# A token router's counting rounds on full 128 by 128 arrays, in a fused attention and mixture-of-experts kernel

## The chip, the cores and the metric

The kernel runs on one core of a Trainium2 chip, as one program. The metric is the device time in microseconds (us) of one launch. Times inside the program are read from one profiled execution, taken by the hardware profiler; "span" is the time from its first to its last instruction. Engines are named as in the profile: PE (matrix multiplies), PEld (the loading of the stationary operand, which overlaps PE), DVE (vector engine), ACT (scalar engine), POOL (GpSimd), SP (the queue that issues most transfers).

## What is computed

Attention through 32 memory slots per head gives 4608 tokens of 512 features. A router then hands every token to one of eight experts with room for 576 tokens each, each expert is a two-layer network, and a dense two-layer network follows.

```python
def _moe_ref(x, w_gate, w1, w2):
    N, D = x.shape
    E = w_gate.shape[1]                 # 8
    cap = N // E                        # 576
    logits = x @ w_gate
    order = np.argsort(-logits.flatten())
    assigned, counts = -np.ones(N, np.int64), np.zeros(E, np.int64)
    for idx in order:                   # best logit first
        tok, e = idx // E, idx % E
        if assigned[tok] >= 0 or counts[e] >= cap:
            continue
        assigned[tok] = e
        counts[e] += 1
    ...
    for e in range(E):
        mask = assigned == e
        out[mask] = np.maximum(x[mask] @ w1[e], 0.0) @ w2[e]
    return out

def _moe2_ref(x, w_in, w_out):
    h = x @ w_in
    return (h * np.clip(h + 3.0, 0.0, 6.0) / 6.0) @ w_out
```

## The kernel before

**Stages.** The first 180 us or so are attention. What follows is recorded by a planner: `mm` (L617, L618) emits one matmul of the expert or dense layers and moves a model clock `CK.now` on by the cost that `fp16` gives; after each matmul, `run` lets background tasks (Python generators) emit their instructions once the model clock has reached the time that each has yielded. So every engine executes in order a stream that the planner wrote, and the costs in the code (`CK.now += 0.3`, `HOP`, `LATE`) set where a task's instructions stand in it. L567 is the helper through which the tasks' DVE, ACT and POOL instructions go, L618 that of the matmuls.

**The main stream on PE.** For each pair P of experts come `l1`, `l2` of expert 2P, `l1`, `l2` of expert 2P+1 (192 matmuls each of 288 columns, written to the tiles `p` from `xt` or `h`), and then `l34`, the dense network on these 1152 tokens. `l34` takes 48 steps; a step is twelve matmuls of 384 columns (`p<-yt,wi`) and nine of 512 columns (`acc<-wo,h`). The dense weights are turned from fp32 bit patterns into scaled pairs of fp16 by the task `dense_piece` (32 pieces, four DVE instructions on the tile `cva` for each) in the first pair's time.

**The router.** `routes` runs `route(k)` for k = 0 to 7, one after the other; `R_OK` lets k = 1 start at the beginning of the experts, 2 and 3 in `l34` of the first pair, 4 and 5 in that of the second, 6 and 7 in that of the third. A route finds the expert that fills up at the highest threshold and the tokens that it takes. Routes 0 to 6 do so in eight rounds (`NST`): in a round, DVE compares the best logit `V` of each token (128 partitions by 36 token tiles) with 15 thresholds `TH` (the tile `C`), PE counts for each threshold and expert how many tokens pass (`C` against the one-hot choice `Bo`), DVE asks which counts reach 576 (`FL`), PE sums those flags and copies the sum to all partitions (`p2`), and DVE makes the next 15 thresholds from it. Route 0 has rounds of 36 small matmuls (L785). From route 1 on a round has three groups on PE:

- L795: nine matmuls, each with four token tiles, 60 columns of `C` as the stationary operand and 32 columns of `Bo` moving; the 15 by 8 blocks on the diagonal of the 60 by 32 result hold the counts of four tile groups;
- L804: four matmuls that add these blocks, with slices `idh` of an identity (60 partitions by 15), after DVE has copied the result out of the accumulator as `CS` (L800);
- L813: one matmul of 15 partitions, ones against `FL`.

After the rounds the route counts once more (L855), which gives the expert's number and lets `weights` fetch its weights (`w_issue`, on the POOL queue); it then ranks its tokens (L882, L883) and makes their index list (six groups L952). `gathers` fetches the tokens' rows by this list (`xg`) and transposes them on PE (`xp`, L623) to the tiles `xt` that `l1` reads; it does so for expert k once `l1` of expert k-1 is emitted. For k of two and more, `LATE` (1.6) adds slack to the planned times: half of it before each L795 group.

## Time and profile before

| | us |
|---|---|
| median of 3 runs | 1510.31 (1505.42, 1511.45, 1510.31) |
| the profiled execution itself | 1503.65 |
| its span, first to last instruction | 1501.6 |
| PE busy in the span | 1397.4 (93%) |
| DVE busy | 835.3 (56%) |
| ACT busy | 732.6 (49%) |
| POOL busy | 487.8 (32%) |

The profiled execution took 2.05 us more than its span, and lies 6.7 us (0.4%) under the median of the three runs. PE is the engine with the largest share, but shares are averages over stages: before 180 us (attention) and from there to about 437 us PE has gaps, after that nearly none. A row of the timeline gives start, duration, engine, line, what is written from what, and in square brackets how long the engine had been idle and for whom it waited. The duration of a merged row of matmuls runs to the end of the last one, which overlaps the next row's start; what a group takes from the stream is therefore read from starts.

### The profile page before, as it was taken

The page shows a single profiled execution, that of the slowest core. Times are in us where ns is not written, and L with a number is a line of the kernel's source. Part 1 is how long each engine was busy: PE and PEld are TensorE (multiplying, and loading weights), DVE is VectorE, ACT ScalarE, POOL GpSimd, SP SyncE. Part 2 cuts the span into 40 slices and gives each one's busy share as a digit, 9 for nine tenths or more (in the row PEclk, how much of TensorE's full clock was granted, in tenths as well). Part 3 has the DMA queues.
Part 4 walks back from the last instruction along what each step waited for, and adds up shares of the span by engine and source line. Part 5 has one row for each costly group of instructions (what it writes and reads, how often), then busy time and mean ns, then how long its engine had stood idle before and what let it go on. Part 6 is the DMA issues. An engine that isn't in the chain of part 4 may idle for free.

```text
span 1501.6 us, 26275 instructions
## 1 busy us (share of the span) xinstructions
PE 1397.4 (93%) x10506; PEld 931.4 (62%) x10506; DVE 835.3 (56%) x1985; ACT 732.6 (49%) x1419; POOL 487.8 (32%) x555
## 2 busy tenths in 40 slices
PE   4778886898889999999999999999999999999997
PEld 3667764777444555997555558875555588755553
DVE  4788967889995775553146755522459335221111
ACT  3667655577763563452335634523346445233332
POOL 3565305134553443301233532102325421023232
PEclk9989996999999999999999999999999999999999
DMA  9866587355310221200001311100013211000000
GB/s 299 293 231 201 158 273 248 118 185 167 114 43 22 82 84 57 86 28 2 1 22 57 109 57 51 64 1 1 22 57 110 71 39 62 1 0 22 1 21 21
DMA packets 65913, 130.67 MB, mean 87 GB/s; under 512 B 5248, under 2 KB 35968, under 8 KB 65792
## 3 DMA queue, kind: packets, MB, share of 16 engines
q1 hardware_dynamic: 49808, 74.48, 15.0%
q0 software_dynamic: 15168, 52.96, 10.9%
q8 instruction: 82, 1.34, 0.4%
q10 hardware_dynamic: 816, 1.57, 0.3%
q14 instruction: 39, 0.32, 0.1%
HBM read 110.12 MB, written 18.87 MB: 86 GB/s over the span
## 4 chain that ended last, share of the span: by engine, by line
PE 67%; DVE 14%; ACT 5%; issue 5%; DMA 4%; POOL 2%; SPq 0%; ACTq 0%; POOLq 0%; DVEq 0%
PE p L618 39%; PE acc L618 21%; DVE cva L567 4%; DMA xg<-xd,ix 2%; PE xa L420 1%; DMA ph<-in_phi_dram 1%; PE kvp L191 1%; DMA wst<-in_moe_w_dram,ei 1%; DVE w L567 1%; ACT h L567 1%; PE rtp L795 1%; DVE pm L138 1%; PE xp L623 1%; DVE h L567 1%; POOL h L567 1%
## 5 line engine op out<-in xcount | busy, mean ns | idle before, releaser
L618 PE MATMUL acc<-wo,h 128*128 128x512 f16 x1728 | 418.1, 379 | 5.2 <-ACT h L567 4.3
L618 PE MATMUL p<-yt,wi 128*128 128x384 f16 x2304 | 417.6, 327 | 0.0
L567 POOL TENSOR_TENSOR h<-h,h 128x384 f16<-128x384 f32 x192 | 187.3, 976 | 634.5 <-ACT h L567 492.6
L618 PEld LDWEIGHTS <-w 128*128 128x128 f16 x3072 | 339.1, 121 | 49.1 <-issue 4.4
L618 PEld LDWEIGHTS <-wi 128*128 128x128 f16 x2304 | 219.2, 98 | 156.0 <-issue 1.2
L567 ACT ACTIVATE h<-p,half_c,inv 128x384 f32<-128x384 f32 (+1 forms) x256 | 143.9, 587 | 278.5 <-PE p L618 271.2
L618 PEld LDWEIGHTS <-h 128*128 128x128 f16 x1728 | 163.5, 98 | 174.1 <-ACT h L567 6.0
L567 DVE SCALAR_TENSOR_TENSOR h<-h,p 128x384 f32<-128x384 f32 x192 | 105.9, 551 | 290.0 <-ACT h L567 282.7
L618 PE MATMUL p<-xt,w 128*128 128x288 f16 x1536 | 198.8, 289 | 3.7 <-DVE h L567 3.5
L618 PE MATMUL p<-h,w 128*128 128x288 f16 x1536 | 196.3, 287 | 4.3 <-DVE w L567 3.7
L567 ACT ACTIVATE h<-h 128x384 f16<-128x384 f32 x192 | 100.1, 521 | 135.7 <-DVE h L567 131.9
L567 DVE SCALAR_TENSOR_TENSOR h<-p,h 128x288 f16<-128x288 f32 x128 | 57.4, 455 | 73.6 <-ACT h L567 73.5
L567 DVE SCALAR_TENSOR_TENSOR w<-wst,s,w 128x512 f16<-128x512 f32 x124 | 96.1, 806 | 2.2 <-ACT w L567 2.2
L567 POOL DMA_INDIRECT wst<-in_moe_w_dram,ei x64 | 68.7, 1073 | 87.0 <-DVE scn L567 33.5
L567 ACT ACTIVATE h<-p 128x288 f16<-128x288 f32 x128 | 51.7, 410 | 90.8 <-PE p L618 90.8
L567 ACT ACTIVATE w<-wst,s 128x512 f16<-128x512 f32 x124 | 82.5, 712 | 7.1 <-DVE s L567 6.2
L567 DVE SCALAR_TENSOR_TENSOR cva<-dst,cva 128x512 int32<-128x512 int32 (+1 forms) x96 | 82.7, 881 | 0.5 <-ACT dst L567 0.3
L567 DVE TENSOR_REDUCE ym<-y 128x1 f32<-128x288 f32 x64 | 28.8, 450 | 91.5 <-ACT y L567 91.3
L567 ACT ACTIVATE wscr<-wst 128x1024 bf16<-128x1024 f32 x64 | 67.3, 1052 | 13.3 <-DMA wst<-in_moe_w_dram,ei 12.6
L567 ACT ACTIVATE y<-p 128x288 f32<-128x288 f32 x64 | 26.1, 407 | 96.6 <-PE p L618 95.1
L567 POOL DMA_INDIRECT xg<-xd,ix x35 | 37.2, 1064 | 75.9 <-PE xp L623 49.7
L191 PE MATMUL kvp<-kvt,A 128*64 128x128 f32 x576 | 46.0, 315 | 7.3 <-ACT A L170 3.3
(313 smaller groups left out, 1558.4 us busy)
## 6 DMA issues: line engine op xcount, KB each, us to landing
dst<-in_moe_w_out_dram SPq DMA_DIRECT2D x26, 512.0 KB, 4.3
qt<-in_q_dram SPq DMA_DIRECT2D x8, 1024.0 KB, 11.5
dq<-in_moe_w_in_dram SPq DMA_DIRECT2D x16, 512.0 KB, 5.7
xd<-xs SPq DMA_DIRECT2D x32, 256.0 KB, 5.5
kvt<-in_k_dram SPq DMA_DIRECT2D x7, 1152.0 KB, 9.1
kvt<-in_v_dram SPq DMA_DIRECT2D x7, 1152.0 KB, 11.8
dst<-in_moe_w_in_dram SPq DMA_DIRECT2D x15, 512.0 KB, 4.0
ph<-in_phi_dram SPq DMA_DIRECT2D x8, 576.0 KB, 9.8
```

The source lines that it names most:

```text
L138: nc.vector.tensor_reduce(pm, PH[b].rearrange("p h (r m) -> p h m r", m=M), axis=AX.X, op=OP.max)
L191: nc.tensor.matmul(p[i * 64:(i + 1) * 64, g, 0:128], A[:, hp, r, :], KV[b][:, :, hp, r * 64:(r + 1) * 64], start=(r == 0), stop=(r == R - 1))
L420: nc.tensor.matmul(p[r, g], AT[u][:, half, g, r], VB[b][:, g], start=True, stop=True)
L567: r = f(*a, **kw)
L618: nc.tensor.matmul(o, l, r, start=start, stop=stop)
L623: nc.tensor.transpose(o, i, idn)
L795: nc.tensor.matmul(p[:60, :32], C[:, 4 * t:4 * t + 4].rearrange("p t n -> p (t n)"), Bo[:, 4 * t:4 * t + 4].rearrange("p t e -> p (t e)"), ...
```

## The change

Counting groups from route 1 on are made eight token tiles wide, with sixteen columns of `C` for each tile in place of fifteen; `C` and `Bo` are padded with zeros to 40 tiles, allocated once and cleared once on POOL. Five matmuls with a stationary operand of 128 by 128 and 64 moving columns take the place of nine. DVE no longer copies the result: it multiplies it by a mask `MK` that keeps the diagonal blocks (`CM`) and adds the eight blocks of a row (`CR`). One matmul with `S8`, a 128 by 128 matrix that adds the tiles, takes the place of four. The flags and the last matmul of a round use all 128 partitions. The planner's costs for the groups go from 0.3 and 0.11 to 0.14 and 0.03, and the second group gets `LATE / 2` of slack as well. Route 0 keeps its matmuls, with `C` read at a stride of 16.

```diff
-    idh = rt.tile([128, 60], F16, name="idh")
-    nc.vector.tensor_copy(idh, ident[:, 0:60])
-    CS = rt.tile([128, 32], F16, name="CS")
+    NTP = 40
+    S8 = rt.tile([128, 128], F16, name="S8")
+    nc.vector.memset(S8, 0.0)
+    MK = rt.tile([128, 8], F16, name="MK")
+    with nc.allow_low_precision(reason="zeros and ones"):
+        nc.vector.tensor_reduce(S8[:, 0:16], ident.rearrange("p (t n) -> p n t", t=8), axis=AX.X, op=OP.add)
+        nc.vector.tensor_reduce(MK, ident.rearrange("p (t n) -> p t n", t=8), axis=AX.X, op=OP.add)
+    CM = rt.tile([128, 8, E], F16, name="CM")
+    CR = rt.tile([128, E], F16, name="CR")
+    C = rt.tile([128, NTP, 16], BF16, name="C")
+    nc.gpsimd.memset(C, 0.0)
+    Bo = rt.tile([128, NTP, E], BF16, name="Bo")
+    nc.gpsimd.memset(Bo, 0.0)
...
-    ones72 = rt.tile([128, 2 * NT], F32, name="ones72")
-    nc.vector.memset(ones72, 1.0)
...
-                    for t in range(9):
-                        nc.tensor.matmul(p[:60, :32], C[:, 4 * t:4 * t + 4].rearrange("p t n -> p (t n)"),
-                                         Bo[:, 4 * t:4 * t + 4].rearrange("p t e -> p (t e)"),
-                                         start=(t == 0), stop=(t == 8))
-                    CK.now += 0.3
+                    for t in range(0, NTP, 8):
+                        nc.tensor.matmul(p, C[:, t:t + 8].rearrange("p t n -> p (t n)"),
+                                         Bo[:, t:t + 8].rearrange("p t e -> p (t e)"),
+                                         start=(t == 0), stop=(t == NTP - 8))
+                    CK.now += 0.14
                     yield CK.now + HOP
-                    V_.tensor_copy(CS[:60], p[:60, :32])
-                    yield V_.t + HOP
+                    V_.tensor_tensor(CM, p.rearrange("p (t e) -> p t e", t=8),
+                                     MK[:, :, None].to_broadcast([128, 8, E]), op=OP.mult)
+                    with nc.allow_low_precision(reason="integers up to 1152"):
+                        V_.tensor_reduce(CR, CM.rearrange("p t e -> p e t"), axis=AX.X, op=OP.add)
+                    yield V_.t + HOP + LATE / 2
                     p1 = ps.tile([128, 64], F32, name="rtp")
-                    for t in range(4):
-                        nc.tensor.matmul(p1[:15, :E], idh[:60, 15 * t:15 * t + 15], CS[:60, E * t:E * t + E],
-                                         start=(t == 0), stop=(t == 3))
-                    CK.now += 0.11
+                    nc.tensor.matmul(p1[:, :E], S8, CR, start=True, stop=True)
+                    CK.now += 0.03
                     yield CK.now + HOP
-                V_.tensor_scalar(FL[:15], p1[:15, :E], float(CAP), None, op0=OP.is_ge)
+                r = slice(0, 128 if k else 15)
+                V_.tensor_scalar(FL[r], p1[r, :E], float(CAP), None, op0=OP.is_ge)
...
-                nc.tensor.matmul(p2[:, :E], onesb[:15], FL[:15], start=True, stop=True)
+                nc.tensor.matmul(p2[:, :E], onesb[r], FL[r], start=True, stop=True)
```

On DVE, one round of a route in `l34` stood like this before (`h` is the dense layer's own work, `CS` the copy, `FL` the flags, `mi` the sum read back):

```order
L567 TENSOR_REDUCE mi<-rtp 128x1
L567 SCALAR_TENSOR_TENSOR TH<-mi,TP 128x15
L567 TENSOR_TENSOR C<-V,TH 128x540
L567 TENSOR_SCALAR fp<-mi,fp 128x1
L567 SCALAR_TENSOR_TENSOR h_6117<-h_6117,p_6073 128x384
L567 CAST CS<-rtp 60x32
L567 TENSOR_SCALAR FL<-rtp 15x8
```

and stands like this now, with two instructions in the place of the copy:

```order
L567 TENSOR_REDUCE mi<-rtp 128x1
L567 SCALAR_TENSOR_TENSOR TH<-mi,TP 128x15
L567 TENSOR_TENSOR C<-V,TH 128x36x15
L567 TENSOR_SCALAR fp<-mi,fp 128x1
L567 SCALAR_TENSOR_TENSOR h_6087<-h_6087,p_6054 128x384
L567 TENSOR_TENSOR CM<-rtp,MK 128x64
L567 TENSOR_REDUCE CR<-CM 128x8
L567 TENSOR_SCALAR FL<-rtp 128x8
```

On PE, the last index group of route 3 stood before among the last dense matmuls of the first pair (`acc`), ahead of the long run of expert 2's `l1` (`p<-xt`):

```order
L618 MATMUL acc_6992<-wo_5887,h_7703 128x512
L952 LDWEIGHTS OH
L952 MATMUL rtp<-RH,OH 128x10
...
L618 LDWEIGHTS h_7703
L618 MATMUL acc_6993<-wo_5887,h_7703 128x512
L618 LDWEIGHTS w_0_6732
L618 MATMUL p_7809<-xt,w_0_6732 128x288
```

and stands now inside that `l1`:

```order
L618 LDWEIGHTS w_2_6712
L618 MATMUL p_7741<-xt,w_2_6712 128x288
L960 LDWEIGHTS OH
L960 MATMUL rtp<-RH,OH 128x10
...
L618 LDWEIGHTS w_3_6743
L618 MATMUL p_7741<-xt,w_3_6743 128x288
```

Counted in matmuls of L618 from the first one, that group moved from behind number 1799 to behind number 1893, and the first transpose of expert 3 stands behind number 1971 in both. Route 2's last index group moved from 1419 to 1460, route 1's from 317 to 300. Expert 2's last transposes moved from behind number 1520 to behind 1567; its `l1` begins behind 1758 in both.

## Rows read from the trace of the kernel before

**Rows 1.** The profile's page: engines, busy us, share, instructions.

```profile
PE 1397.4 (93%) x10506; PEld 931.4 (62%) x10506; DVE 835.3 (56%) x1985; ACT 732.6 (49%) x1419; POOL 487.8 (32%) x555
```

**Rows 2.** Stretches: start:end, length, then busy us of each engine, granted clock, DMA.

```profile
437.00:600.00 163.00, 159.47 (x1067) 83.18 (x1066) 103.64 (x269) 79.29 (x147) 65.47 (x67) 1.00 0.17 57
600.00:1130.00 530.00, 529.00 (x3711) 349.52 (x3710) 247.93 (x632) 223.48 (x439) 133.06 (x141) 1.00 0.12 39
1130.00:1260.00 130.00, 126.33 (x871) 86.83 (x870) 65.17 (x136) 65.64 (x123) 48.72 (x49) 1.00 0.26 81
340.00:437.00 97.00, 84.44 (x528) 54.12 (x527) 96.09 (x150) 71.84 (x133) 50.89 (x39) 0.96 0.39 124
237.00:293.00 56.00, 41.20 (x330) 33.59 (x330) 45.16 (x123) 29.47 (x56) 12.39 (x12) 0.80 0.50 163
```

**Rows 3.** One line's instructions: shortest, median, longest ns; first and last start.

```profile
L795 PE MATMUL rtp<-Bo,C x432: 181/181/233, 239.8 to 1106.1; 128*60 128x32 bf16 x144
```

**Rows 4.** PE's timeline around route 6: clean starts of dense steps.

```profile
1054.41 2.11 PE L618 MATMUL acc<-wo,h 128*128 128x512 f16 x9
...
1066.09 2.11 PE L618 MATMUL acc<-wo,h 128*128 128x512 f16 x9
...
1108.91 2.11 PE L618 MATMUL acc<-wo,h 128*128 128x512 f16 x9
```

**Rows 5.** PE's timeline, last round of route 6: the matmul of 15 rows.

```profile
1107.38 0.99 PE L618 MATMUL p<-yt,wi 128*128 128x384 f16 x5
1108.30 0.17 PE L813 MATMUL rtp<-FL,onesb 15*128 15x8 bf16 x1
1108.41 0.66 PE L618 MATMUL p<-yt,wi 128*128 128x384 f16 x3
```

**Rows 6.** PE's timeline right behind: small matmuls of the full array.

```profile
1110.85 1.14 PE L618 MATMUL p<-yt,wi 128*128 128x384 f16 x6
1111.83 0.17 PE L855 MATMUL rtp<-ce,onesb 128*128 128x8 bf16 x1
1111.85 1.14 PE L618 MATMUL p<-yt,wi 128*128 128x384 f16 x6
...
1120.01 0.29 PE L952 MATMUL rtp<-RH,OH 128*128 128x10 bf16 x6
1120.16 0.81 PE L618 MATMUL p<-yt,wi 128*128 128x384 f16 x4
```

**Rows 7.** One line's weight loads: ns shortest, median, longest.

```profile
L952 PEld LDWEIGHTS <-OH x282: 95/96/99, 229.2 to 1171.9; 128*128 128x128 bf16 x141
```

**Rows 8.** DVE's timeline: a masked multiply, a reduction (attention), the router's copy.

```profile
160.16 0.23 DVE L291 TENSOR_TENSOR vg<-misc,mask 128x64 f32<-128x64 f32 x1
160.42 0.26 DVE L292 TENSOR_REDUCE VG<-vg 128x16 f32<-128x64 f32 x1
...
1106.34 0.18 DVE L567 CAST CS<-rtp 60x32 f16<-60x32 f32 x1 [0.48 <-PE rtp L795]
```

**Rows 9.** DVE groups from 345 to 437 us: count, busy us, mean ns.

```profile
L567 DVE SCALAR_TENSOR_TENSOR cva<-dst,cva 128x512 int32<-128x512 int32 (+1 forms) x66 | 58.1, 905 | 0.1
L567 DVE TENSOR_SCALAR cva<-dst 128x512 int32<-128x512 int32 x22 | 15.8, 718 | 0.0
```

**Rows 10.** A POOL clear; DVE's wait at the router's constants; route 0's first counts.

```profile
L108 POOL MEMSET km<- x16: 516/520/525, 21.3 to 137.0; 64x512 f16 x16
192.10 0.18 DVE L679 TENSOR_SCALAR tab<-tid 128x36 int32<-128x36 int32 x1 [0.34 <-POOL tid L676]
197.10 1.05 PE L785 MATMUL rtp<-Bo,C 128*15 128x8 bf16 x36
```

**Rows 11.** PE's timeline: route 3's end, expert 3's first transposes; a gather on the chain.

```profile
605.09 0.30 PE L952 MATMUL rtp<-RH,OH 128*128 128x10 bf16 x6
...
626.41 0.60 PE L623 MATMUL xp<-ident,xg 128*128 128x128 f32 x4
...
318.65 4.43 DMA xg<-xd,ix
```

More of the change, by code (lines that the diff above doesn't have):

```diff
@@ L741, in route @@
         bm = rt.tile([128, NT], F32, name="bm")
-        Bo = rt.tile([128, NT, E], BF16, name="Bo")
         def best(c0, c1):
@@ L753, in cmp @@
         def cmp(C, TH, c0, c1):
-            V_.tensor_tensor(C[:, c0:c1], V[:, c0:c1, None].to_broadcast([128, c1 - c0, 15]),
+            V_.tensor_tensor(C[:, c0:c1, 0:15], V[:, c0:c1, None].to_broadcast([128, c1 - c0, 15]),
                              TH.bitcast(F32)[:, None, :].to_broadcast([128, c1 - c0, 15]), op=OP.is_ge)
@@ L764, in route @@
             for i in range(NST):
-                C = rt.tile([128, NT, 15], BF16, name="C")
                 p = ps.tile([128, 64], F32, name="rtp")
@@ L784, in route @@
                         for t in range(c0, c1):
-                            nc.tensor.matmul(p[:15, :E], C[:, t], Bo[:, t], start=(t == 0), stop=(t == NT - 1))
+                            nc.tensor.matmul(p[:15, :E], C[:, t, 0:15], Bo[:, t], start=(t == 0), stop=(t == NT - 1))
                         CK.now += 0.0243 * (c1 - c0)
@@ L848, in route @@
         BC = rt.tile([128, E, NT], F32, name="BC", tag="BC")
-        V_.tensor_tensor(BC, Bo.rearrange("p t e -> p e t"), G[:, 0, None, :].to_broadcast([128, E, NT]), op=OP.mult)
+        V_.tensor_tensor(BC, Bo[:, :NT].rearrange("p t e -> p e t"), G[:, 0, None, :].to_broadcast([128, E, NT]), op=OP.mult)
         ce = rt.tile([128, E], BF16, name="ce")
@@ L873, in route @@
         sc = rt.tile([128, 2, NT], F32, name="scn")
-        V_.tensor_tensor_scan(sc.rearrange("p a t -> p (a t)"), ones72, G.rearrange("p a t -> p (a t)"), 0.0,
+        V_.tensor_tensor_scan(sc.rearrange("p a t -> p (a t)"), ones_c[:, 0:2 * NT], G.rearrange("p a t -> p (a t)"), 0.0,
                               op0=OP.mult, op1=OP.add)
```

## The prediction

> **What bounds the kernel now.** I read the table of stretches first, because the shares of the page [rows 1] are means over stages with different limits. From 437 us on, PE is the limit: it is busy 159.5 of 163 us, then 529.0 of 530, then 126.3 of 130, at a granted clock of 1.00, that is 2.4 GHz [rows 2]. What leaves PE's stream there shortens the program by as much; what only makes another engine's chain longer costs nothing until PE waits for it. Before that it is otherwise. From 340 to 437 us DVE is busy 96.1 of 97 us and PE 84.4 [rows 2]: DVE is the limit, with the conversion of the dense weights. From 237 to 293 us, route 1's time, DVE is busy 45.2 and PE 41.2 of 56 us at a mean clock of 0.80 [rows 2]: a stage of waits between the two.
>
> The router's rounds lie in both. L795 has 432 matmuls, nine a round, so 48 rounds, eight in each of routes 1 to 6 [rows 3]. Route 1 begins its eight at 239.8 us, in the stage of waits; the 40 of routes 2 to 6 follow in the first three `l34`, the last at 1106.1 us [rows 3], where PE is the limit.
>
> **What a round takes from PE's stream now.** The durations of the small matmuls do not tell, since they overlap; starts do. From 1054.41 to 1066.09 us there are three clean steps of the dense layer (twelve `p`, nine `acc`), 3.893 us each. From 1066.09 to 1108.91 us stand nine such steps and the eight rounds of route 6 [rows 4]. 42.82 - 9 x 3.893 = 7.78 us, or 0.973 us a round.
>
> The rows beside it say why that is so much for 14 tiny matmuls. The one of 15 rows, L813: six `p` take 0.98 us from 1110.85 to 1111.83 [rows 6], 0.163 each, so the five from 1107.38 should free the array at 1108.20; L813 starts at 1108.30 and the next `p` at 1108.41 [rows 5]. It costs 0.21 us, half of it idle array ahead of it. The matmul L855 with the same eight columns but all 128 rows starts where the `p` before it ends and is followed after 0.02 us; six of L952 with ten columns, 128 by 128, take 0.15 us together [rows 6], 0.025 each. So a small matmul of full shape slides into the stream, and one of partial shape holds the stream on both sides of it.
>
> **The change on PE.** A round loses its three partial groups, 0.973 us. It gains five matmuls of 128 by 128 with 64 columns and two with eight. By the nearest rows the two cost 0.03 each (L855, rounded up). For the five the trace has no row of this width; bounds are the 0.025 of ten columns, and, if the stationary loads would not overlap at all, the 0.096 us that one load of 128 columns shows as its duration [rows 7]. I take 0.030: in `p` a column costs 0.163 / 384 = 0.0004 us, so 64 columns need 0.027, next to the lower end, and the six loads of L952 in 0.15 us show that loads do overlap. The group is then 0.15, the round 0.21, and the saving 0.76 us a round; over 40 rounds **30.4 us**. The bounds give 0.973 - 0.185 = 0.79 (31.5 us) and 0.973 - 0.54 = 0.43 (17.3 us).
>
> **The change on DVE.** A round loses the copy, 0.18, and gains a masked multiply out of the accumulator on 128 by 64, 0.23 by the same instruction in attention, and a reduction of 64 elements, 0.26 [rows 8]: +0.31 us. The comparison `C` has the same 540 elements. In routes 2 to 6 that is 12.4 us of an engine busy 64% or less [rows 2], so it costs nothing by itself; it sits in the chain of a round, and behind it on DVE wait the dense layer's `h`, which PE's `acc` reads. In route 1 it is 2.5 us more on a DVE that is the limit soon after.
>
> **Route 1's stage, 237 to 437 us.** For it: PE gets 8 x 0.76 = 6.1 us less to do there. Against it: 2.5 us more DVE work, and one dense piece fewer stands ahead of the first dense steps than before; a piece is 3 x 0.905 + 0.718 = 3.4 us of DVE [rows 9], which then falls where DVE is full. I take the ends, -6 and +6 us, and the middle, 0: an earlier start of the DVE-bound stretch and more work in it cancel as far as these rows can tell.
>
> **The start.** The two clears on POOL, 640 and 320 elements, cost 0.65 and 0.33 us by the 0.52 for 512 [rows 10]; they stand ahead of the `tid` table, for which DVE already waited 0.34 us, so route 0's DVE work moves by some 1.0 us (this also covers the new constants on DVE, estimated at 0.5 from the 0.26 of rows 8). Route 0's first counts started on PE with no wait [rows 10], so some of that is covered: +0.5 us, half; bounds 0 and 1.
>
> **Later index lists.** The planner now gives a round more time, mostly the new slack of 0.8. Route 3's last index group stands 94 matmuls of `l1` later (`p` of 288 columns, 0.122 us each): 11.5 us. Before, that group began at 605.09 and expert 3's first transposes at 626.41 [rows 11], 21 us later. The gather between takes two issues and a transfer of 4.4 us [rows 11], estimated 7.5 us in all. So 13.8 us of cover are there and 11.5 are used; 0 us, but with about 2 us left, in two places (experts 3 and 5). For experts 2, 4 and 6 the transposes follow their own list closely, but `l1` comes late: 191 matmuls of the dense mix stand between expert 2's last transposes and its `l1`, at 3.893 / 21 = 0.185 us each, 35 us.
>
> **Sum.** 1503.65 - 30.4 + 0 + 0.5 = **1473.8 us** against the profiled execution's own time. That one lies 6.7 us under the median of the runs; against the median the sum would be 1480.4. I state the middle, 1477 us.
>
> **Rivals.** (1) *The wider loads bind.* Each of the five matmuls needs a new stationary operand of 128 columns, where nine of 60 went before. If loads did not overlap, the five cost 0.48 and the saving is 17.3 us: 1487 us. For it: the 96 ns of rows 7. Against it: rows 6, six such loads in 0.15 us. The Trainium skill, page "TensorE: Matmul & The Clock Gate", section "LDWEIGHTS (loading the stationary operand)", counts a load by its columns over 1.2 GHz, and so speaks against this change: 107 ns for each of 128 columns, five of them 0.53 us, an estimate by which the round would still be 0.38 us cheaper and the program 15 us. The trace agrees with that figure as a duration (96 ns) and not as a cost in the stream (25 ns).
>
> (2) *The price is not the shape but the handover.* If each group pays for interrupting the stream, whatever its shape, only the seven matmuls fewer are saved: 7 x 0.025 = 0.18 us a round, 7 us, 1497 us. Against it: L855 interrupts the same stream for 0.02 us. This is also the case in which the change does not do what it says.
>
> (3) *DVE's stretch before 437 us grows.* The +6 us above: 1480 us against the profiled time, 1486 against the median.
>
> (4) *Slower: the router comes too late.* Its rounds now take longer in the plan; if the cover of the lists were not there, PE would wait 11.5 us for the rows of experts 3 and 5 and 41 matmuls of the dense mix, 7.6 us, for each of 2, 4 and 6: +46 us, 1520 us. Against it: the 13.8 and 35 us of cover. It decides from the point where a list comes over 14 us later; to lose the whole gain, 15 us more for each of experts 3 and 5 are needed.
>
> **Chances.** A measurement of this kernel can tell about 0.5% (7.5 us) from no change. Forecast (PE's saving arrives, route 1's stage within a few us of nothing) 0.72; rival 3 0.11; rival 1 0.08; rival 2 0.05; rival 4 0.04. Forecast and rivals 1 and 3 are faster; rival 2 lies at the edge and goes to no change. Faster 0.92, no change 0.05, slower 0.03. The range: from below, 31.5 us saved on PE and 6 in route 1's stage, 1466, with 2 for the runs' spread, 1464; from above, rival 3 against the median, 1486, and rival 1, 1487 or 1494 against the median: 1490.
>
> **What would show it.** Route 6's eight rounds and nine steps from clean start to clean start: 8 x 0.21 + 35.0 = 36.7 us in place of 42.8 (for as many steps as it then spans, 0.21 a round). A group of five followed by the next dense matmul after 0.15 us, with no gap ahead of it; the single matmuls after 0.03. If the gap stays, rival 2; if the five take 0.5, rival 1. DVE between 340 and 437 us still full, and PE's waits there longer or not: rival 3. A wait of PE for the rows `xg` ahead of expert 3's or 5's transposes of more than 1 us each: rival 4. The prediction is wrong if PE from 437 us on shows idle time that it did not have, above all before `xp` or behind `CM`.

## The result, and the profile after

The changed kernel takes 1482.36 us, the median of six runs (1478.17 to 1487.09); the kernel before, run beside it, 1505.99 us (six runs, 1501.62 to 1511.45). The ratio is 0.9836, 95% interval 0.9808 to 0.9864: 1.6% faster. The time lies inside the predicted range, 5 us over the predicted 1477. The profiled execution of the changed kernel took 1484.15 us and has a span of 1482.4; that is 19.5 us under the profiled execution of before.

The page's row of engines, against [rows 1]: PE loses 336 instructions (48 rounds times seven matmuls) and 28 us of busy time, DVE gains 30 us.

```profile
PE 1369.2 (92%) x10170; PEld 927.2 (63%) x10170; DVE 865.4 (58%) x2034; ACT 732.3 (49%) x1419; POOL 495.9 (33%) x561
```

Two of the stretches of [rows 2] (start:end, length, busy us of PE, PEld, DVE, ACT, POOL, granted clock, DMA):

```profile
600.00:1130.00 530.00, 523.31 (x3632) 352.08 (x3630) 275.94 (x684) 233.64 (x459) 145.45 (x150) 1.00 0.13 42
...
340.00:437.00 97.00, 82.94 (x516) 54.56 (x515) 96.27 (x151) 72.18 (x134) 52.52 (x37) 0.91 0.41 131
```

Two things stand in them. PE is still the limit in the long stretch, but it now idles 6.7 us there where it idled 1.0. And from 340 to 437 us DVE is full as before, while the granted clock of TensorE is 0.91 where it was 0.96.

**The rounds themselves.** PE's timeline of route 6, against [rows 4 to 6]: start, duration, line, what is written from what, and in brackets idle time and for whom.

```profile
1053.93 2.11 PE L618 MATMUL acc<-wo,h 128*128 128x512 f16 x9
1055.88 0.81 PE L618 MATMUL p<-yt,wi 128*128 128x384 f16 x4
1056.53 0.31 PE L801 MATMUL rtp<-Bo,C 128*128 128x64 bf16 x5
1056.67 1.46 PE L618 MATMUL p<-yt,wi 128*128 128x384 f16 x8
...
1062.85 1.89 PE L618 MATMUL acc<-wo,h 128*128 128x512 f16 x8 [0.33 <-DVE y L567]
...
1097.06 0.17 PE L812 MATMUL rtp<-CR,S 128*128 128x8 f16 x1
1097.09 0.97 PE L618 MATMUL p<-yt,wi 128*128 128x384 f16 x5
1097.90 0.17 PE L821 MATMUL rtp<-FL,onesb 128*128 128x8 bf16 x1
1097.93 1.14 PE L618 MATMUL p<-yt,wi 128*128 128x384 f16 x6
1098.90 2.11 PE L618 MATMUL acc<-wo,h 128*128 128x512 f16 x9
```

Four `p` from 1055.88 end at 1056.53, where the group of five starts at once; the next `p` starts 0.14 us later. The single matmuls take 0.03. From 1053.93 to 1098.90 stand eleven dense steps and eight rounds: 44.97 - 11 x 3.893 - 0.33 (the wait shown) = 1.82 us, or 0.227 a round where 0.973 was. The saving is 0.746 us a round, 29.8 us over 40 if the other four routes are like route 6.

**Where the time went, by stage.** The matmuls `amx<-ident,sy_1m`, `sy_3m`, `sy_5m` and `sy_7m` (a step in preparing the weights of experts 1, 3, 5, 7) stand once in each kernel and cut the program: routes 2 and 3 run between the first two, 4 and 5 between the next, 6 before the last. The first and the last of them on PE's timeline, of before and of the changed kernel:

```profile
390.09 0.77 PE L694 MATMUL amx<-ident,sy_1m 128*128 128x128 f32 x2 [5.45 <-DVE sy_1m L567]
...
1312.23 0.38 PE L694 MATMUL amx<-ident,sy_7m 128*128 128x128 f32 x2
```

```profile
393.89 0.77 PE L702 MATMUL amx<-ident,sy_1m 128*128 128x128 f32 x2 [5.99 <-DVE sy_1m L567]
...
1292.58 0.38 PE L702 MATMUL amx<-ident,sy_7m 128*128 128x128 f32 x2
```

Up to `sy_1m` the changed kernel is 3.8 us later. From `sy_1m` to `sy_7m` it needs 898.7 us where 922.1 were needed: 23.4 of the 29.8 us arrive, 6.4 are given back. The waits of PE between 450 and 1300 us say to whom (us in total, times, longest), of before:

```profile
PE xp L623 <- DMA xg<-xd,ix: 2.1, 4, 1.0
PE rtp L855 <- DVE ce L567: 1.7, 1, 1.7
PE rtp L795 <- DVE C L567: 1.2, 3, 0.5
PE acc L618 <- DVE y L567: 0.4, 1, 0.4
```

and in the same view of the changed kernel:

```profile
PE xp L623 <- DMA xg<-xd,ix: 4.0, 4, 2.6
PE acc L618 <- DVE y L567: 3.6, 6, 1.0
...
```

With five smaller ones (4.1 us) these are 11.7 us, where all of before are 5.4: 6.3 more, which is the size of the part given back. Between `sy_1m` and 450 us one wait took the place of others: PE now stands 2.9 us for POOL's `h`, where it stood 4.3 us for ACT's `h` in four pieces. The experiments ask two things: whether the saving is due to the shape, and why those waits came.

### The profile page after: what moved, and what is told of

It reads as the page before. It is cut to its first block, busy times and chain, and to the rows that moved or that the text cites. A ratio compares the mean times of both kernels' runs of the same rounds, so it can differ in the third digit from the quotient of the medians.

```text
span 1482.4 us, 25640 instructions
## 1 busy us (share of the span) xinstructions
PE 1369.2 (92%) x10170; PEld 927.2 (63%) x10170; DVE 865.4 (58%) x2034; ACT 732.3 (49%) x1419; POOL 495.9 (33%) x561
## 4 chain that ended last, share of the span: by engine, by line
PE 63%; DVE 17%; issue 6%; ACT 6%; DMA 5%; POOL 3%; SPq 0%; ACTq 0%; POOLq 0%; DVEq 0%
PE p L618 38%; PE acc L618 18%; DVE cva L567 4%; DVE w L567 2%; PE xa L420 2%; DMA wst<-in_moe_w_dram,ei 2%; DMA xg<-xd,ix 2%; DVE h L567 1%; POOL h L567 1%; PE kvp L191 1%; ACT w L567 1%; ACT h L567 1%; DMA kvt<-in_v_dram 1%; DVE pm L138 1%; PE xp L623 1%
## 5 line engine op out<-in xcount | busy, mean ns | idle before, releaser
L618 PE MATMUL acc<-wo,h 128*128 128x512 f16 x1728 | 415.7, 380 | 8.3 <-DVE y L567 3.6
L618 PE MATMUL p<-yt,wi 128*128 128x384 f16 x2304 | 411.8, 327 | 0.0
L618 PEld LDWEIGHTS <-w 128*128 128x128 f16 x3072 | 339.6, 122 | 51.5 <-DVE w L567 5.3
L618 PEld LDWEIGHTS <-wi 128*128 128x128 f16 x2304 | 220.9, 98 | 162.7 <-issue 4.1
L618 PEld LDWEIGHTS <-h 128*128 128x128 f16 x1728 | 163.9, 98 | 178.5 <-issue 5.9
L618 PE MATMUL p<-xt,w 128*128 128x288 f16 x1536 | 200.8, 290 | 2.5 <-DVE h L567 2.2
L618 PE MATMUL p<-h,w 128*128 128x288 f16 x1536 | 196.6, 288 | 5.6 <-DVE w L567 4.6
L567 ACT ACTIVATE wscr<-wst 128x1024 bf16<-128x1024 f32 x64 | 67.4, 1052 | 17.1 <-DMA wst<-in_moe_w_dram,ei 16.2
```

What stands on the lines that cost most here:

```text
L567: r = f(*a, **kw)
L618: nc.tensor.matmul(o, l, r, start=start, stop=stop)
```

## Experiments

The kernels of a group (rows 3 to 6, 7 to 10 and 11 to 14 of the table) ran on one chip, beside the same runs of the kernel before. The three profiles of the changed kernel show how far the last two columns vary for one kernel: 2 and 3 us. "Sum" below is the time from `sy_1m` to `sy_7m`, and "`sxm` to `sy_1m`" that from the matmuls `amx<-ident,sxm` (at 198.6 us in before) on, each from the starts in that kernel's trace.

| kernel | median us (runs) | ratio to before, 95% | `sxm` to `sy_1m` | sum |
|---|---|---|---|---|
| before, first profile | | | 191.5 | 922.1 |
| changed, first profile | 1482.36 (6) | 0.9836 (0.9808 to 0.9864) | 194.6 | 898.7 |
| changed, again | 1484.22 (5) | 0.9862 (0.9840 to 0.9884) | 194.6 | 897.8 |
| before, flags on 128 rows | 1497.37 (12) | 0.9952 (0.9931 to 0.9972) | 190.9 | 914.3 |
| before, nine of 128 columns | 1497.01 (12) | 0.9946 (0.9929 to 0.9963) | 191.0 | 913.5 |
| changed, route 1 as before | 1479.80 (5) | 0.9844 (0.9821 to 0.9867) | 193.6 | 894.8 |
| changed, 120 columns | 1487.56 (4) | 0.9880 (0.9849 to 0.9911) | 192.7 | 903.8 |
| changed, no second slack | 1485.61 (6) | 0.9865 (0.9842 to 0.9889) | 192.8 | 901.5 |
| changed, route 0 too | 1486.00 (5) | 0.9856 (0.9837 to 0.9875) | 201.9 | 894.4 |
| changed, more slack | 1511.58 (10) | 1.0033 (1.0015 to 1.0051) | 192.1 | 927.8 |
| changed, a third time | 1483.64 (5) | 0.9835 (0.9817 to 0.9854) | 192.5 | 900.7 |
| route 1 as before, again | 1481.46 (5) | 0.9813 (0.9796 to 0.9830) | 193.6 | 894.7 |
| changed, rows later | 1476.53 (5) | 0.9787 (0.9768 to 0.9806) | 192.7 | 892.9 |
| both | 1475.57 (5) | 0.9785 (0.9769 to 0.9801) | 193.2 | 890.6 |

### Is it the shape?

**The kernel before, with its 15-row matmul made 128 rows deep**, and nothing else:

```diff
+    nc.vector.memset(FL, 0.0)
...
-                nc.tensor.matmul(p2[:, :E], onesb[:15], FL[:15], start=True, stop=True)
+                r = slice(0, 128 if k else 15)
+                nc.tensor.matmul(p2[:, :E], onesb[r], FL[r], start=True, stop=True)
```

> Before, with one part of the change alone: the last matmul of a round (L813) takes all 128 rows of the flags, of which rows 15 to 127 are zero. The same number of matmuls at the same places. Theory (a partial shape holds the stream on both sides): its cost in the stream falls from 0.21 to 0.03 us, 0.18 x 40 = 7.2 us less, 0.995 of before. Rival (the handover costs, whatever the shape): no change, 1.000.

1497.37 us against 1505.26: 0.5% less, and the interval of the ratio (0.9931 to 0.9972) excludes no change. PE's timeline there:

```profile
1092.77 0.99 PE L618 MATMUL p<-yt,wi 128*128 128x384 f16 x5
1093.59 0.17 PE L815 MATMUL rtp<-FL,onesb 128*128 128x8 bf16 x1
1093.62 0.81 PE L618 MATMUL p<-yt,wi 128*128 128x384 f16 x4
```

Five `p` of 0.163 us from 1092.77 end at 1093.59. The matmul starts there and costs 0.03, where with 15 rows it cost 0.21 [rows 5]. The number of matmuls and their order are those of before; only the rows differ. The sum fell by 7.8 us, 0.196 in each of 40 rounds.

The weight loads (PEld) show what the partial shape does to the stream: first in the kernel before, behind the five `p` of [rows 5], then in this one.

```profile
1108.30 0.09 PEld L813 LDWEIGHTS <-onesb 15*128 15x128 bf16 x1 [0.32 <-issue]
1108.40 0.28 PEld L618 LDWEIGHTS <-wi 128*128 128x128 f16 x3
```

```profile
1093.43 0.10 PEld L815 LDWEIGHTS <-onesb 128*128 128x128 bf16 x1
1093.59 0.45 PEld L618 LDWEIGHTS <-wi 128*128 128x128 f16 x4
```

With 128 rows the load begins at 1093.43, 0.16 us ahead of its matmul, while a `p` still runs. With 15 rows PEld stands idle for 0.32 us, the load begins only with its matmul (1108.30), and the load of the next `p` begins behind that (1108.40). In routes 2 to 6 of the kernel before, all 120 partial groups have it so: the first load begins 1 to 5 ns ahead of its matmul. In the 40 full ones of this kernel it begins 160 to 215 ns ahead. The price of a partial shape is a load that is not hidden, on the way in and on the way out.

**The kernel before, with nine matmuls of 128 stationary columns in place of 60.** They still are nine, with 32 moving columns; the upper 64 columns only fill rows of the result that nobody reads. The copy behind it takes 64 rows in place of 60, `idh` has slices at a stride of 16, and `C` is one buffer, padded and cleared once on POOL, as in the changed kernel.

```diff
-                        nc.tensor.matmul(p[:60, :32], C[:, 4 * t:4 * t + 4].rearrange("p t n -> p (t n)"),
+                        nc.tensor.matmul(p[:, :32], C[:, 4 * t:4 * t + 8].rearrange("p t n -> p (t n)"),
```

> Before, with the first group of a round (L795) still nine matmuls of 32 moving columns, but with 128 stationary columns (eight tiles of 16, of which the upper four tiles' results are not used). The two other groups stay partial, nothing moves in the order. Theory (shape): no gap ahead of the group, nine matmuls at 0.025 to 0.03 us, 0.24 in place of 0.46: 0.22 x 40 = 9 us less, 0.994. Rival (handover, or the count of matmuls): 1.000. Rival (loads of 128 columns bind): 9 x 0.096 = 0.86, 0.4 us a round more, 16 us, 1.011.

1497.01 us, again 0.5%. A group with more than twice the stationary columns became cheaper:

```profile
1089.31 0.81 PE L618 MATMUL acc<-wo,h 128*128 128x512 f16 x3
1089.95 0.38 PE L794 MATMUL rtp<-Bo,C 128*128 128x32 bf16 x9
1090.18 1.46 PE L618 MATMUL acc<-wo,h 128*128 128x512 f16 x6
```

Three `acc` of 0.216 end at 1089.96, where the nine start; they take 0.23 us, 0.026 each. The nine of 60 columns cost 0.46 in the kernel before, from the end of eight `acc` at 1105.77 to the next `acc`:

```profile
1104.04 1.89 PE L618 MATMUL acc<-wo,h 128*128 128x512 f16 x8
1105.86 0.44 PE L795 MATMUL rtp<-Bo,C 128*60 128x32 bf16 x9
1106.23 0.39 PE L618 MATMUL acc<-wo,h 128*128 128x512 f16 x1
```

Rival 1 (wider loads bind) falls by this run, and rival 2 (the price is the handover) by both. The third group, four matmuls of 60 rows and 15 columns, was not changed by itself; start to start it costs 0.27 us in the kernel before, and the single matmul in its place 0.03.

**The changed kernel with 120 columns**, the padding column of each token tile left out:

```diff
-    C = rt.tile([128, NTP, 16], BF16, name="C")
+    C = rt.tile([128, NTP, 15], BF16, name="C")
...
-                        nc.tensor.matmul(p, C[:, t:t + 8].rearrange("p t n -> p (t n)"),
+                        nc.tensor.matmul(p[:120], C[:, t:t + 8].rearrange("p t n -> p (t n)"),
```

> The changed kernel with the padding column of each token tile left out: the five matmuls of a round have 120 stationary columns in place of 128 (all 128 rows), the rest is the same; the single matmul behind them keeps its 128 rows, with the last eight rows zero. If a group is cheap because it uses all rows (the shape of e1), the columns do not matter: the five cost 0.15 us as before, the time is that of the changed kernel, 1480 to 1486 us, ratio 0.984 to 0.987. If a group is only cheap where rows and columns are both full, the stream stands still around it again as it did with 60 columns: some 0.2 to 0.3 us a round, 40 rounds, 8 to 12 us more, 1491 to 1496 us, ratio 0.990 to 0.993, and a gap of 0.1 us ahead of each group of five.

1487.56 us; the sum is 903.8, 4.7 over the mean of the three profiles of the changed kernel (899.1). Neither theory holds. The rows show why: first PE's timeline of this kernel, then the durations (shortest, median, longest ns) of the weight loads with 120 columns, with 128 (the changed kernel) and with 60 (the kernel before):

```profile
1057.44 0.81 PE L618 MATMUL p<-yt,wi 128*128 128x384 f16 x4
1058.10 0.41 PE L802 MATMUL rtp<-Bo,C 128*120 128x64 bf16 x5
1058.34 1.47 PE L618 MATMUL p<-yt,wi 128*128 128x384 f16 x8
```

```profile
L802 PEld LDWEIGHTS <-C x240: 128/135/221, 240.6 to 1097.4; 128*120 128x120 bf16 x120
```

```profile
L801 PEld LDWEIGHTS <-C x240: 95/98/151, 242.7 to 1095.1; 128*128 128x128 bf16 x120
```

```profile
L795 PEld LDWEIGHTS <-C x432: 104/110/157, 239.8 to 1106.1; 128*60 128x60 bf16 x144
```

There is no gap ahead of the group (four `p` end at 1058.09), but the five cost 0.25 us in place of 0.145, 0.1 more a round, which is 4 us over 40 rounds. A load of 120 columns takes 135 ns, one of 128 columns 98; the matmuls of the group start 0.055 us apart, where with 128 columns they start 0.029 apart.

So the price has two parts. The first is the load that is not hidden around a group that uses few rows or columns: with 60 columns the stream stands still 0.09 us ahead of the group, and the next dense matmul starts 0.11 us behind its last one, where it starts 0.025 behind with 128 columns. The second is the load that is too slow inside a group: with 120 columns it adds 0.026 us to each matmul. With 60 columns, 110 ns a load, that part is small: from the second matmul on they start 0.030 us apart, and those of 128 columns in the run before 0.025. The Trainium skill has a rule that bears on the second part: its page "TensorE: Matmul & The Clock Gate", section "Weight-path perf modes — Fast Weight Load (FWL) and DoubleRow", says that the fast way of loading weights is on where their number is 128 and the type is not FP32. The trace agrees, 98 against 135 ns. The Trainium skill's section "LDWEIGHTS (loading the stationary operand)" on the same page, by which a load costs in proportion to its columns, does not agree with these three rows.

### What takes back 6 us: the lists

**The changed kernel again**, to see which waits return.

> The changed kernel itself, run again for a second profile and more times. Theory: PE's saving in the rounds (0.75 us each, 40 rounds, 30 us) arrives, and about 6 us are given back elsewhere; time 0.984 of before. Two places of the first profile are asked after. PE's wait of 2.6 us for the rows of expert 4 ahead of the third transposes: if it comes from the order on the POOL queue it stands here again, within 1 us; if it was chance it is gone. The lower granted clock from 223 to 233 us (2 us lost): if it were the change's doing it stands here again; if it was the moment of a pause it is gone or elsewhere.

1484.22 us. PE waits for expert 4's rows again (1.9 us at the longest), and 3.1 us for POOL's product at 420 us. The lower granted clock stands there again too: 0.79 from 220 to 236 us in both profiles, 1.00 in before. But it is 0.89 there in the third profile and in both variants of the kernel before, so it does not come with the change. POOL's timeline of the changed kernel's first profile shows the first:

```profile
830.08 0.95 POOL L567 DMA_INDIRECT xg<-xd,ix  x1 [1.26 <-DVE ix L567]
...
833.39 1.04 POOL L567 DMA_INDIRECT out_dram<-y,ix  x1 [0.17 <-issue]
...
839.80 0.98 POOL L567 DMA_INDIRECT xg<-xd,ix  x1 [0.16 <-issue]
```

and PE's timeline at the same place:

```profile
845.87 0.66 PE L623 MATMUL xp<-ident,xg 128*128 128x128 f32 x4 [2.58 <-DMA xg<-xd,ix]
```

Expert 4's third gather stands on POOL's queue behind three scatters of finished rows and a weight fetch, and is issued at 839.80. PE comes to its transposes at 843.29 and stands for 2.58 us, although `l1` of expert 4, which needs them, is far away. In the kernel before, that gather stands behind one weight fetch and ahead of the scatters (issued at 838.65, landed 3.3 us later), and PE comes 2.4 us after its rows. The place on the queue takes this margin away, but does not make the whole wait: at the same place behind the scatters, the gather lands 4.0 us after its issue in the two profiles with route 1 as before (further down), with waits of 0.3 and 0.4 us, and 5.3 to 5.4 us after it in the second and third profile of the changed kernel, with 1.9. Why it lands later there is open.

**The slack ahead of the single matmul taken out** (before the change there was none at that place).

```diff
-                    yield V_.t + HOP + LATE / 2
+                    yield V_.t + HOP
                     p1 = ps.tile([128, 64], F32, name="rtp")
                     nc.tensor.matmul(p1[:, :E], S8, CR, start=True, stop=True)
```

> The changed kernel without the 0.8 us of slack that the planner gives the single matmul behind CR (before there was none at that place). Each of routes 2 to 6 then ends about 6 us earlier in the stream, route 3's last index group 86 of the dense layer's matmuls earlier. Theory A (the later lists cost the 2 to 3 us that expert 4's third transposes wait for their rows): that wait goes or shrinks under 1 us, and the time falls by 2 to 4 us, 1479 to 1481 us. Theory B (the lists are early enough; expert 4's gather stands behind the output's scatters on POOL's queue): the wait stays at 2 to 3 us, the time is the same within 2 us, or 2 to 8 us longer where PE now waits for CR ahead of the single matmul (up to 0.2 us in each of 40 rounds).

1485.61 us, the changed kernel's time. PE's waits between 820 and 1000 us:

```profile
PE rtp L801 <- DVE C L567: 2.2, 1, 2.2
...
```

The wait for rows shrinks (one of 1.5 us, where 3.2 stood in the changed kernel), and a wait for `C` of 2.2 us takes its place; the sum is 901.5. The earlier lists are paid for with rounds that PE meets too soon. This does not separate the two theories.

**More slack**, 2.4 us in place of 0.8 at the same place.

```diff
-                    yield V_.t + HOP + LATE / 2
+                    yield V_.t + HOP + 1.5 * LATE
```

> The changed kernel with 2.4 us of slack in place of 0.8 ahead of the single matmul behind CR: each of routes 2 to 6 ends about 13 us later in the stream than in the changed kernel. Theory A (rival 4 of the prediction: about 2 us of cover were left for the lists of experts 3 and 5): PE waits for the rows ahead of the first transposes of experts 3 and 5, 10 us each, or the planner moves these transposes behind the list and the dense layer's matmuls that should fill the time are missing later: the time rises by 10 to 25 us, 1494 to 1508 us. Theory B (there was more cover than that): the waits ahead of xp rise by less than 3 us each and the time stays within 5 us, 1480 to 1489 us.

1511.58 us, ratio 1.0033 where the changed kernel has 0.9862 and 0.9835: the whole gain is lost. The slack of routes 2 and 3 adds up, so route 3's list comes not 13 but 29 us later (its last index group at 638.65 us, 609.80 in the second profile of the changed kernel), and PE runs dry behind expert 2:

```profile
638.65 0.30 PE L960 MATMUL rtp<-RH,OH 128*128 128x10 bf16 x6
...
642.26 0.49 PE L702 MATMUL amx<-ident,sy_2m 128*128 128x128 f32 x2 [2.93 <-DVE sy_2m L567]
646.06 1.94 PE L623 MATMUL xp<-ident,xg 128*128 128x128 f32 x8 [3.31 <-ACT yt L567]
650.88 1.08 PE L623 MATMUL xp<-ident,xg 128*128 128x128 f32 x4 [2.89 <-DMA xg<-xd,ix]
```

From `sy_1m` to `sy_3m` it takes 324.2 us where the changed kernel's second profile has 307.2, from there to `sy_5m` 310.9 for 297.3: 17 and 14 us lost. PE's idle time accounts for 9.8 and 8.1 of them. The rest goes with a cost that rival 4 did not count: behind the first of these waits the granted clock is 0.50 (1.2 GHz) for 17.1 us, here and again from 953.7 us, where the changed kernel's second profile has 1.00 (columns as above):

```profile
643.10:660.20 17.10, 8.84 (x34) 6.37 (x35) 10.72 (x24) 14.23 (x27) 3.77 (x4) 0.50 0.38 125
```

This is rival 4 at experts 3 and 5; in the changed kernel itself it stays away from expert 3. There the list ends at 612.11 us and expert 3's first transposes start at 621.86, 9.75 us later, without a wait.

**Rows later**: the planner's slack for a gather of token rows (experts 2 to 7) from 2.2 to 4.2 us. Nothing is added or removed; transposes move behind more of the dense layer's matmuls.

```diff
-                rdy.append(dma(0.75, G_.t) + (2.2 if k > 1 else 0.0))
+                rdy.append(dma(0.75, G_.t) + (4.2 if k > 1 else 0.0))
```

> The changed kernel once more, beside the next three on one chip: 1482 to 1485 us, ratio 0.984 to 0.987, with the wait of expert 4's third transposes for their rows of about 2 us, and of the dense layer's first matmuls for POOL's product of about 3 us.

> The changed kernel with 4.2 us in place of 2.2 as the planner's slack for a gather of token rows (experts 2 to 7); the transposes of expert 4 then stand behind more of the dense layer's matmuls. Theory A (part of the gain is lost because PE meets these transposes before their rows are there): PE's waits of 2 to 3 us for xg between 820 and 1000 us shrink under 1 us and the time falls by 1.5 to 3 us, 1480 to 1482 us. Theory B (the wait only moves: the later rows delay the next gather, which uses the same buffers, or expert 5's): the waits add up to the same 2 to 3 us, or more, and the time is that of the changed kernel within 1.5 us.

1476.53 us against 1483.64 of the changed kernel beside it; the ratios' intervals, 0.9768 to 0.9806 and 0.9817 to 0.9854, do not meet. The gain, 7 us, is over twice what I expected. PE's waits between 450 and 1300 us are now

```profile
PE acc L618 <- DVE y L567: 4.0, 6, 1.1
...
```

No wait for `xg` is left, 6.2 us in all, and the sum is 892.9: 29.2 us under before, where 29.8 had left PE's stream. The third profile of the changed kernel had 5.5 us of waits for `xg`, the second 3.9; the sum is 4.9 to 7.8 us shorter than in its three profiles. Whether the kernel before would also gain by this slack was not run; its own waits for `xg` were 2.1 us.

### Route 1's stage and route 0

**Route 1 as before**, nine matmuls of 64 columns in place of 60 and four of 64 rows in place of 60, flags of 15 rows; routes 2 to 6 in the new form.

```diff
+                    if k == 1:
+                        for t in range(9):
+                            nc.tensor.matmul(p[:64, :32], C[:, 4 * t:4 * t + 4].rearrange("p t n -> p (t n)"),
+                                             Bo[:, 4 * t:4 * t + 4].rearrange("p t e -> p (t e)"),
+                                             start=(t == 0), stop=(t == 8))
...
-                r = slice(0, 128 if k else 15)
+                r = slice(0, 128 if k > 1 else 15)
```

> The changed kernel with route 1 alone as it was: nine matmuls of 64 columns, copy, four matmuls, the matmul of 15 rows; routes 2 to 6 changed. Theory (in route 1's stage the saving on PE and the added work on DVE cancel): the time of the changed kernel within 3 us, 0.984 of before, and the all-partition maximum of expert 1's second layer (sy_1m) at the same time within 2 us of the changed kernel's. Rival (the change loses in route 1's stage what the forecast of 30 us lacks): 4 to 6 us faster than the changed kernel, 0.980, and sy_1m 4 us earlier.

> Route 1 as before, routes 2 to 6 in the new form, once more. Theory A (the new form costs something in route 1's stage, where DVE is the limit): the span from sxm to expert 3's first transposes is 2 to 4 us shorter than in the changed kernel beside it, and the time 2 to 5 us shorter, 1478 to 1481 us. Theory B (the 4 us of the first look are spread of the runs): the times are the same within 1.5 us.

> Route 1 as before and the 4.2 us of slack together. If both theories A hold, the gains add: 4 to 7 us under the changed kernel, 1476 to 1480 us, ratio 0.980 to 0.983, faster than both kernels of this case. If neither holds: 1482 to 1485 us.

1479.80 and 1481.46 us in the two groups, 4.4 and 2.2 under the changed kernel beside it. The intervals overlap, so the times alone do not separate them. The traces agree with each other: the sum is 894.8 and 894.7, against 897.8 to 900.7 in three profiles of the changed kernel. Two things go with it. The waits for `xg` behind 390 us are 1.9 and 2.5 us, where the changed kernel has 3.9 to 5.5. And the wait for POOL at 420 us is missing; the changed kernel shows it on PE's timeline, in the stretch right behind (columns as above), and on POOL's timeline:

```profile
424.81 1.25 PE L618 MATMUL acc<-wo,h 128*128 128x512 f16 x3 [2.94 <-POOL h L567]
425.85 3.41 PE L618 MATMUL p<-yt,wi 128*128 128x384 f16 x12
```

```profile
425.00:430.00 5.00, 5.00 (x20) 2.34 (x19) 5.00 (x6) 2.47 (x5) 5.00 (x4) 0.66 0.43 138
```

```profile
418.83 4.60 POOL L567 TENSOR_TENSOR wi<-cva,wi 128x512 f16<-128x512 f32 x1 [2.10 <-ACT wi L567]
```

POOL's product `h` for this step stands behind that dense conversion of 4.60 us; the kernel's 15 others like it take 1.15 to 2.19 us. PE is idle for 2.94 us, and behind that its granted clock is 0.66 over 5 us and twelve `p` show 3.41 us where they show 2.11 elsewhere. With route 1 as before the conversions stand otherwise and POOL's longest conversion between 404 and 432 us takes 1.46 and 1.47 us in the two profiles. PE stands as long there all the same, 3.7 and 4.1 us for ACT's `h` in three pieces; what is gone is the lower clock behind the wait. From `sy_1m` to `sy_3m` it is 305.4 us in both profiles, against 307.0 to 307.4 in the changed kernel. The stage up to `sy_1m` is not shortened (193.6). Both edits together give 1475.57 us, within 1 us of the slack alone: the gains overlap, since both take away waits for `xg`. The sum, 890.6, is 2.3 us shorter again, which the times do not tell from nothing.

**Route 0 in the new form too**, with `CM`, `CR` and the `S8` matmul in its rounds, counted in parts of 32 and 8 tiles (the first round), then 16 and 24.

```diff
-                        for t in range(c0, c1):
-                            nc.tensor.matmul(p[:15, :E], C[:, t, 0:15], Bo[:, t], start=(t == 0), stop=(t == NT - 1))
-                        CK.now += 0.0243 * (c1 - c0)
+                        count(c0, c1)
+                    V_.t = max(V_.t, CK.now + HOP)
+                    block()
```

> The changed kernel with route 0's 16 rounds in the new form as well: a round's 36 matmuls of one token tile each (15 columns wide) become five of eight tiles, with the masked multiply, the reduction and one more single matmul behind them. If route 0 is bound by PE, 36 x 0.0243 - 5 x 0.03 = 0.72 us fall away a round, at most 11.6 us in all, and sxm comes 5 to 11 us earlier: 1473 to 1479 us. If it is bound by the chain of a round (comparison, counts, threshold, flags), the round loses the wait for the last counts (0.44 us for the second half) and gains 0.23 + 0.27 us on DVE and two handovers between the engines of about 0.2 us: 0.4 to 0.8 us more a round, sxm 6 to 12 us later, and a part of it at the end: 1484 to 1494 us. I hold the second for likelier, 0.6 to 0.4.

1486.00 us: no gain. (Route 0 has eight rounds, not the sixteen of the expectation, so at most 5.8 us were there.) A round takes 3.19 us from one flags' matmul to the next (220.65 to 223.84), where the changed kernel needs 3.21 (219.12 to 222.33). So these rounds are bound by the chain between the engines: PE's time fell, and in six of the eight rounds it now stands some 0.4 us for `CR`. `sxm` did not come later, as I had thought; the loss stands in route 1's stage, 201.9 us where 192 to 195 are usual, which was not followed further.

## Why the prediction was right, and where it was not

- **What bounds.** PE as the limit from 437 us on: right. But the sign that I had named for a wrong prediction, new idle time of PE ahead of `xp`, did appear, 6.3 us of it with what stands behind DVE.
- **The price of a round.** 0.21 forecast, 0.227 measured; the five 0.15 and 0.14, the singles 0.03 and 0.03. Of 30.4 us forecast, 29.8 left the stream. Two parts show alone, by the sums: 0.196 a round by the flags' rows, 0.216 by the nine matmuls' columns (8.6 us over 40). Start to start they are 0.175 and 0.24.
- **The reason for it.** Shape, as forecast: a partial group holds the stream on both sides, because its load and the load behind it do not overlap the matmul ahead. But there is a second part that I had not seen: inside a group, loads of 120 columns cost more than loads of 128. I had read the absence of the load's price from L952 [rows 6, 7] without asking on which width that depends. It made no difference to the sum, since the change pads to 128; with 120 columns it is 4 us.
- **DVE's 0.31 us a round.** `CM` takes 0.22 and `CR` 0.27, less 0.18 for the copy: 0.31, right. "It costs nothing by itself" was mis-sized: at six places PE waits for the accumulator's read-out `y`, 3.6 us where 0.4 stood. The rows below show one of the smallest of them (0.33, the wait at 1062.85 above), first DVE, then POOL. `y` stands on DVE behind a round's thresholds and its `C`, and the thresholds took 0.89 us (0.23 in the clean case, as at 839.71) while POOL worked on `h`. In all DVE's busy time grew by 30 us and the new instructions make 15 of it; the rest is what instructions that got longer have over those that got shorter. The change shifted the phase of the rounds against the dense steps, and that has a price which I did not look for. The planner's slack moves it: without the second slack one wait for `y` is left (0.9 us), with more slack none, though both kernels lose elsewhere what that gives. With the slack for rows the 4.0 us for `y` are still there.

```profile
1060.49 0.89 DVE L567 TENSOR_SCALAR TH<-KT,fp 128x15 int32<-128x15 int32 x1
...
1062.06 0.75 DVE L567 TENSOR_SCALAR y<-acc,inv 128x512 f32<-128x512 f32 x1
```

```profile
1060.44 0.91 POOL L567 TENSOR_TENSOR h<-h,h 128x384 f16<-128x384 f32 x1 [2.60 <-ACT h L567]
```

- **Later index lists.** For experts 3 and 5, "0 us, with about 2 us left" holds: 9.75 us between list and transposes where I estimated a need of 7.5, first transposes without a wait, later ones 0.6 each (up to 0.5 in the second profile; 0.2 and, for expert 5, 2.2 in the third, where rival 4's sign does show once); and more slack loses 17 and 14 us in the first two pairs. The step that failed is the next one. I gave experts 2, 4 and 6 35 us of cover because `l1` comes late. That covers `l1`, not the transposes: these stand in PE's stream right behind the list, PE executes in order, and it waited 2.58 us there for a gather that had fallen behind the scatters on POOL's queue and landed late. Rows later shows what this costs: without these waits the sum gives 29.2 us.
- **Route 1's stage.** Taken as 0 with ends of 6 us. From `sxm` to `sy_1m` before and its two variants need 190.9 to 191.5 us, the changed kernel (three profiles) and its variants with the same route 1 (four) 192.1 to 194.6: 2 us more. It is not the new form of route 1, for with the old one it is 193.6. New constants, the shared `C` and the plan remain; this stays open. Rival 3, DVE's stretch before 437 us, shows in part: one conversion fewer stands early, POOL's late product replaces ACT's waits, and the clock falls. Up to the 205th `p` of the dense layer, ahead of route 2's first round in every kernel, the changed one needs 259.5 to 261.6 us from `sxm` (three profiles), before 257.0: 2.5 to 4.6 us more, where rival 3 had 6 and the sum had 0.
- **The start.** 0.5 us cannot be told: `sxm` lies between 196.5 and 202.9 us over all these kernels.
- **The sum.** -29.8 on PE, +6.3 in waits after 450 us, +3.8 up to `sy_1m`, of which 0.7 at the start: -19.7; measured -19.65 at the start of the last dense matmuls (1487.61 and 1467.96) and -19.5 in the profiled times. It closes to some 1.5 us and no better, since from `sy_1m` to route 2 the changed kernel loses another 1.4 us that is not in it. Against the medians the gain is 21 to 24 us.
- **Luck.** The sum forecast 1473.8 us for the profiled time, and 1484.15 was measured. Of the 10 us between, 6.3 are the new waits after 450 us, which stand in no term of the sum and in no bound of the range: its upper end, 1490, came from rivals 1 and 3. That the time lies inside is in that part luck.

## What to carry to other kernels

Give a small matmul that is put into a dense stream all 128 rows and exactly 128 stationary columns, padded with zeros if need be; what it computes in vain cost nothing here, while 14 matmuls of partial shape cost 0.75 us a round more than the seven full ones. When a list or a gather moves, look for the first instruction of an in-order engine that reads it, not for the first work that needs its result; that instruction is where the engine stops. And after a gain that shifts a stream, read the new waits group by group: one number of the planner gave back a quarter of this gain.

## What the hardware showed

- A weight load of 60 columns took longer (110 ns) than one of 128 (98 ns), and one of 120 longest (135 ns), all bf16 with 128 rows. Inside a group the matmuls started 0.030 us apart with 60 columns, 0.025 to 0.029 with 128 and 0.055 with 120.
- The load of a group with 15 or 60 rows, or with 60 columns, never began ahead: 1 to 5 ns before its matmul in 120 of 120 cases. Those of 128 rows with 120 or 128 columns mostly began 0.16 to 0.21 us ahead.
- One idle stretch of 2.94 us on PE was followed by a granted clock of 0.66 over the next 5 us, with 1.3 us lost on twelve matmuls. All six profiles with that wait for POOL have a lower clock behind it, and none of the other eight has one there. In "more slack", 17.1 us at 0.50 began right behind a wait of 2.93 us, twice.
- A small DVE instruction stretches beside POOL. In the 14 traces, DVE's thresholds `TH<-KT,fp` of 15 elements took 0.23 to 0.30 us in the 69 cases with no product of POOL beside them, and 0.89 to 1.60 us in the 29 cases with one. On the other side, POOL's product at 418.83 us took 4.60 us (4.61 and 4.60 at this place in two more profiles of the changed kernel) while DVE worked without a break; but most of the 15 others also ran beside a busy DVE, in 1.15 to 2.19 us, so what makes this one so long is not shown. The Trainium skill, page "GPSIMD Engine Reference", section "1. Specifications", says that POOL shares its SBUF interfaces with VectorE, with contention for some DVE instructions; the rows of `TH` agree, and give no rule for which other instructions pay.
